# Last attention quad of a fused attention and MLP block: its own token order with large P·V groups, two more pieces of the output projection inside it

## Chip, core and metric

One core of one Trainium2 chip. The number that counts is the device time of one execution, in microseconds (us), as the median of the runs; less is better. TensorE multiplies matrices into PSUM, VectorE, ScalarE and GpSimd (POOL) work element by element, SyncE (SP) issues the transfers.

## What is computed

```python
h = _layernorm(x) * (1 + ca) + sa              # x: 2048 x 576, float32
q = (h @ wq) as 32 heads of 18;  k = h @ wk;  v = h @ wv      # one key and one value head for all
p = softmax(q k^T * 18 ** -0.5)
x = x + ga * ((p v as 2048 x 576) @ wo)
h = _layernorm(x) * (1 + cb) + sb
y = _layernorm(h)
x = x + gb * (gelu(y @ w1 + b1) @ w2 + b2)     # hidden size 4608
```

The six vectors sa, ca, ga, sb, cb, gb come from one small product of a conditioning vector.

## The kernel before, in words

The queries are cut into 4 blocks of 512 tokens and the heads into 8 groups of four, which makes 32 "quads" (n = 0 to 31). For each quad the kernel makes 64 score tiles of 128 keys by 512 queries (token S0 or S1, `st_mm` at line 927: one matmul into a PSUM bank, then one Exp on ScalarE into a tile P), and 64 unit products with V (token V with a number, `pv_mm` at line 914: four matmuls side by side on the columns of the array, one unit is 128 of 512 query columns). 16 chunks of 128 keys make a quad; the products with V run eight units behind the scores (`LAG`), so a quad's last two chunks are multiplied in the next quad. Beside this, a quad also makes the row maxima of the next quad (M and X/R tokens, on VectorE). The last quad has no next one, so it has no maxima.

Each engine runs its instructions in the order in which the program issues them, and that order is written out by hand as a string of tokens: `QUAD`, `QUADW`, and for the last quad `LAST` and `LASTW`, strung together in a loop (lines 894, 895 and 989). The loop at line 980 goes through the quads and walks their tokens. PSUM has 8 banks in this stage: `psB` four, `psM` three, `psC` one (the accumulator of P·V). A score tile takes the next bank of psB or psM, and TensorE can be at most as many scores ahead of ScalarE as there are banks.

After a quad's last P·V, `post_quad` (line 733) goes through five steps, one at each of the tokens T1, RC, T2, OS: ScalarE copies O out of psC, VectorE transposes it, the rows are divided by their sum, VectorE transposes back, and OS splits O into a high part (ScalarE, line 757) and a low part (line 758, POOL for all quads but the last) and sends both with four transfers (line 762) into the tile `ATT` (named big in the profile), which the output projection reads.

The output projection (`wo_mm`, line 711) makes 128 tokens by 288 columns per piece. Token WO runs one whole piece (14 matmuls) of the first three token blocks; 24 such pieces are spread over the later quads, the last two of them at the very end of quad 30 and in the middle of quad 31. The fourth block's pieces have five row groups k = 0 to 4 with three matmuls each; k = 0 to 3 need the quads up to 30, k = 4 only quad 31. They run in `wo_tile` (line 1065), which opens the MLP stage: three token tiles with k = 0 to 3 (72 matmuls) cover the five steps of the last quad, then k = 4 for the same tiles (18 matmuls), then the MLP's first products. During these steps `form` (line 1045) makes the MLP's operands: "+X" is a rounding copy on ScalarE, "=X" a difference on VectorE, "-X" the remainder on VectorE, which needs both. `todo` (line 1082) says which of them stand between the steps of the last quad.

Of the kernel before, what the change touches and what calls it, by code (L numbers as in the profile page):

```python
# [15 lines left out]
NB = 4  # L16
TB = S // NB
NT = TB // 128
KD = 5
NQ = H // 4  # L20
NQT = NB * NQ
# [11 lines left out]
def block_kernel(ctx: ExitStack, tc, x, wqkv, wo, w1, b1, w2, b2, c, wmod, ident_in, out):  # L33
    nc = tc.nc
    ve, ac, po, pe, sy = nc.vector, nc.scalar, nc.gpsimd, nc.tensor, nc.sync
# [15 lines left out]
    def psA(): return PS["t"].tile([128, 2, 512], F32, name="psA", bufs=2)  # L51
    def psM(): return PS["t"].tile([128, 512], F32, name="psM", bufs=3)
    def psB(): return PS["t"].tile([128, 512], F32, name="psB", bufs=PS["b"])
# [392 lines left out]
    for tb in range(NB):  # L446
        nz = big() if tb + 1 < NB else None
        for i, m in enumerate((4, 0, 1, 2, 3)):
# [27 lines left out]
            if tb < 2:  # L476
                for _ in range(NSTAT[tb][i]):
                    ln1_stats(*stats.popleft())
                for _ in range(NAPPLY[tb][i]):
                    b, t = applies.popleft()  # L480
# [13 lines left out]
    WO, YR, ATT, B2 = {}, {}, {}, {}  # L494
# [140 lines left out]
    def ln2_rows(tb, t):  # L635
        if "b" not in B2:
            B2["b"] = load_b2()
            yield
            b2_scaled(B2["b"])
        if tb % 2 == 0 and t == 0:  # L640
            YR[tb // 2] = per.tile([128, 2 * KD, TB], F32, name="yr", tag="big", bufs=3)
        yield from ln2_tile(tb, t)
        if tb % 2 and t == NT - 1:
            R = YR[tb // 2]
            po.tensor_tensor(R[:, 5:7], R[:, 7:9], R[:, 5:7], op=ALU.subtract)
            yield
            po.tensor_tensor(R[:, 5:7], R[:, 5:7], R[:, 0:2], op=ALU.add)
            yield
# [59 lines left out]
        po.tensor_tensor(R[:, 5:7], R[:, 5:7], R[:, 0:2], op=ALU.add)  # L708
        yield

    def wo_mm(tb, t, h2, p, k0, k1):
        A = ATT[tb]
        cs = slice(288 * h2, 288 * (h2 + 1))
        for k in range(k0, k1):
            w = 128 if k == KD - 1 and tb == NB - 1 else 126
            ah, al = (A[:w, i, 128 * t:128 * (t + 1)] for i in (k, KD + k))
            wh, wl = (WO[i][:w, k, cs] for i in "hl")
            if k < KD - 1 or tb == NB - 1:
                terms = [(ah, wh), (ah, wl), (al, wh)]
            else:  # L720
                terms = [(ah, wh), (al[:5 * DH], wl[:5 * DH])]
            for i, (a, b) in enumerate(terms):
                pe.matmul(p[:, :288], a, b, start=(k == 0 and i == 0), stop=(k == KD - 1 and i == len(terms) - 1))  # L723

    def wo_add(tb, t, h2, p):
        X = XT[:, NT * tb + t, 288 * h2:288 * (h2 + 1)]
        ve.tensor_tensor(X, p[:, :288], X, op=ALU.add)

    def wo_piece(tb, t, h2, p):
        wo_mm(tb, t, h2, p, 0, KD)  # L730
        wo_add(tb, t, h2, p)
# [46 lines left out]
    def load_w1(i, what):  # L778
        for w in what.split():
            a = 4 * OPS.index(w) if w in OPS else 28  # L780
            b = min(a + 4, 31)
            sy.dma_start(W1["r"][:, a:b].bitcast(F32), w1scr[i, :, a:b])
# [86 lines left out]
    def tail_parts(o, tail, d, e=po):  # L869

        e.tensor_tensor(d, tail[:, 0], tail[:, 1], op=ALU.subtract)
        for x, y in ((o[:, :2], tail), (o[:, 2], d)):
# [18 lines left out]
            M0 S1 OS S0 M1 WO S0 R1 M1 S0 M1 S0 X1 V3 S0 M1 M0 S1 S1 M1 S0 V3 M0 S1 S0 R1 S0 M0 X1 V3 M0 S1  # L891
            X1 M0 S1 M0 S1 V4 S1 M0 R1 S0 M1 S0 V4 S0 M1 M0 F1 S1 S0 S1 V4 M0 S1 M0 X1 S0 M1 F2 V4 M1 S0 S0
            S1 M0 S1 M0 V3 R1 S0 S0 S1 R1 M0 V3 S0 S1 M0 S1 M0 S1 V3 M0 S1 M1 S0 M1 S0 V3""".split()
    LASTW = "S0 S1 S0 S1 S0 S1 WO V4 S0 S1 V4".split()
    LAST = "S0 S1 S0 S1 V4 S0 S1 S0 S1 V4".split()
    P, PVt = {}, {}
    posts = []
    fill = deque([late_weights()])
# [1 line left out]
    def step(q):  # L900
        if q:
            try:
                return next(q[0])
            except StopIteration:
                q.popleft()
# [8 lines left out]
    def pv_mm(n, kc, h0, h1):  # L914

        if kc == 0 and h0 == 0:
            PVt[n] = psC()
        t = P.pop((n, kc)) if h1 == 4 else P[n, kc]
        cs = slice(128 * h0, 128 * h1)
        for j in range(4):  # L920
            pe.matmul(PVt[n][32 * j:32 * (j + 1), cs], V[:, kc, :], t[:, j, cs],  # L921
                      start=(kc == 0 and h0 == 0), stop=(kc == 15), skip_group_check=True)
        if kc == 15 and h1 == 4:
            posts.append(post_quad(n, PVt.pop(n)))
            next(posts[0])

    def st_mm(n, kc, g, i, ps):
        if (n, kc) not in P:
            P[n, kc] = pb.tile([128, 4, TB], F32, name="P", bufs=4)
        t = ps()  # L930
        pe.matmul(t, KS[64 * g:64 * g + 64, 128 * kc:128 * (kc + 1)], QST[n][64 * g:64 * g + 64, i, :],  # L931
                  start=True, stop=True)
        ac.activation(P[n, kc][:, 2 * i + g, :], t, AF.Exp, scale=SCALE)  # L933
# [21 lines left out]
    def between(n, kc):  # L955

        if kc == 1 and n >= 1 and n + 2 < NQT:
            load_q(n + 2)
        if kc % 2 and (held[0] != "T" or not pieces):
            held[0] = step(fill)  # L960
        if n > 3 and kc not in quiet:
            for _ in range(1 + (kc % 4 != 3)):
                step(prep)
        if kc == 8 and n == NQT - 1:
            while prep:
                step(prep)
# [3 lines left out]
    def wo_next(ps):  # L970
        tb, t, h2 = pieces.popleft()
        wo_piece(tb, t, h2, ps())
        for _ in range(2):
            if held[0] == "T":
                held[0] = step(fill)
        if h2 and tb < 2:
            fill.append(ln2_rows(tb, t))

    pq = 0
    for n in range(NQT):  # L980
        ns = [0, 0]
        if n < NQT - 1:
            order = QUADW if n > NQ else QUAD
            if n == NQT - 2:
                order = order + ["WO"]
        else:
            order = []
            for d in range(8):
                order += LASTW + ["RW"] if d == 4 else LAST
                order += {1: ["T1"], 2: ["RC"], 4: ["T2"], 5: ["OS", "V4"]}.get(d, [])  # L990
        if n < NQT - 1:
            kf, kr = (sum(int(tok[1]) for tok in order[:order.index(a)] if tok[0] == "V") // 4 for a in ("F2", "RC"))
            quiet = kf - 2, kf - 1, kr - 1
        for tok in order:
            if tok[0] == "V":
                g = int(tok[1])
                while g:
                    i = min(g, 4 - pq % 4)
                    if pq >= LAG:
                        pv_mm(*divmod((pq - LAG) // 4, 16), pq % 4, pq % 4 + i)  # L1000
                    pq, g = pq + i, g - i
                    if pq % 4 == 0:
                        between(*divmod(pq // 4 - 1, 16))
            elif tok[0] == "S":
                g = int(tok[1])
                st_mm(n, ns[g] // 2, g, ns[g] % 2, psM if ns[g] % 2 and (n == NQT - 1 or n == NQT - 2 and ns[g] > 24) else psB)
                ns[g] += 1
            elif tok in maxima:
                unit = next(maxima[tok], None)
                if unit:  # L1010
                    mx_mm(*unit, tok[0], int(tok[1]))
            elif tok == "WO":
                wo_next(psB)
            elif tok == "RW":
                for i, w in enumerate("hl"):
                    sy.dma_start(WO[w][:, KD - 1, :].bitcast(F32), woscr[i])
            elif tok[0] == "F":
                (smax_fin1 if tok == "F1" else smax_fin2)(n + 1)
            elif n:
                if next(posts[0], 0) == 0:  # L1020
                    posts.pop()
        if n == NQT - 1:
            W1["r"] = per.tile([128, 40, 128], F32R, name="w1a", tag="big", bufs=3)
            load_w1(0, " ".join(OPS) + " tails")
# [38 lines left out]
    wop = {}  # L1063

    def wo_tile(t, k0, k1):
        if t not in wop:
            p = psA() if t != 2 else None
            wop[t] = [psB()[:, :288] if t == 2 else p[:, h2, :288] for h2 in range(2)], p
        for h2 in range(2):
            wo_mm(NB - 1, t, h2, wop[t][0][h2], k0, k1)  # L1070
        if k1 == KD:
            o, p = wop[t]
            if p is None:
                for h2 in range(2):
                    wo_add(NB - 1, t, h2, o[h2])
            else:
                Xv = XT[:, NT * (NB - 1) + t, :].rearrange("p (a b) -> p a b", a=2)
                ve.tensor_tensor(Xv, p[:, :, :288], Xv, op=ALU.add)

    for t in range(3):  # L1080
        wo_tile(t, 0, KD - 1)
    todo = deque(("+B11 +T2", "-B11 =T3 +B21 +T3", "-T2 -T3", "-B21"))
    form(todo.popleft())
    for _ in posts.pop():
        form(todo.popleft())
# [7 lines left out]
    for t in range(3):  # L1093
        wo_tile(t, KD - 1, KD)
# [410 lines left out]
```

## Time and profile before

| | |
|---|---|
| median of 3 runs | 2228.65 us (2228.53 to 2231.1) |
| span of the profiled execution | 2225.7 us, 2.95 us under that median; the page gives no other time for it |
| TensorE busy | 2207.4 us (99%) |
| VectorE, ScalarE, POOL busy | 1931.9, 1639.8, 1527.0 us |
| Exp of the scores, ScalarE (L933) | 2008 of 621 ns |
| last quad | about 1337 to 1373.8 us in the span |

A busy TensorE is not a TensorE at its peak: a matmul counts as busy while it sits in the pipeline, so the table's 99% says little about a stage. In the rows, a number in brackets is the engine's idle time before the instruction and what released it; "x4" is a merged run of four instructions, whose time runs from the first start to the last end. PEld is the weight load that goes before each matmul; it waits where the matmul would.

### The profile page before, as it was taken

To read this page: it belongs to the slowest core of one execution; us is meant where nothing else is said; L and a number is where in the kernel's file an instruction comes from. 1 tells how busy PE (TensorE), PEld (TensorE's weight loads), DVE (VectorE), ACT (ScalarE), POOL (GpSimd) and SP (SyncE) were. 2 spreads that over 40 slices of the span, in tenths; PEclk is the share of its full clock that TensorE was granted. 3 is DMA by queue.
4 is the path that set the end of the run, shared out by engine and by line. 5 is a ranking of instruction groups with operands and counts; after the bars stand their busy time and mean duration, and the time that the engine had idled before them with its cause. 6 is when DMAs were issued, how large, how long until landed. Compare 5 with 4: busy or idle time off the path is not lost.

```text
span 2225.7 us, 46108 instructions
## 1 busy us (share of the span) xinstructions
PE 2207.4 (99%) x16630; PEld 1451.2 (65%) x16630; DVE 1931.9 (87%) x3415; ACT 1639.8 (74%) x3145; POOL 1527.0 (69%) x1761
## 2 busy tenths in 40 slices
PE   8999999999999999999999999999999999999999
PEld 6654544444544445454454545888888898989898
DVE  7589999999999999999999983887888878888887
ACT  5569999999999999999999997444444444343443
POOL 6653455666776687677676631888888867877776
PEclk9999999999999999999999999999999999999999
DMA  6232143433333333333333322666666646676664
GB/s 231 85 131 92 34 135 115 139 125 119 127 119 114 115 129 105 107 126 111 126 123 117 115 70 63 205 178 175 178 179 180 185 129 182 180 218 188 177 185 124
DMA packets 184776, 308.00 MB, mean 138 GB/s; under 512 B 19711, under 2 KB 75407, under 8 KB 184549
## 3 DMA queue, kind: packets, MB, share of 16 engines
q1 hardware_dynamic: 184405, 304.91, 44.3%
q8 instruction: 132, 2.16, 0.4%
q14 instruction: 95, 0.78, 0.1%
q10 hardware_dynamic: 144, 0.15, 0.0%
HBM read 200.97 MB, written 93.79 MB: 132 GB/s over the span
## 4 chain that ended last, share of the span: by engine, by line
PE 93%; ACT 1%; DVE 1%; issue 0%; ACTq 0%; DVEq 0%
PE psC L921 24%; PE psB L1144 18%; PE psA L1247 16%; PE psB L931 14%; PE psM L319 12%; PE psB L723 2%; PE psB L941 2%; PE psA L1281 1%; PE psA L723 1%; ACT P L933 1%; PE psB L155 0%; PE psB L248 0%; PE psB L357 0%; PE psM L931 0%; DVE mx L344 0%; DVE mx L337 0%
## 5 line engine op out<-in xcount | busy, mean ns | idle before, releaser
L933 ACT ACTIVATE P<-psB 128x512 f32<-128x512 f32 x2008 | 1051.1, 621 | 43.8 <-PE psM L319 20.0
L953 DVE TENSOR_REDUCE mx<-psM 128x1 f32<-128x512 f32 x1476 | 934.3, 682 | 29.9 <-PE psM L319 12.9
L931 PE MATMUL psB<-qst,KS 64*128 64x512 f32 x2008 | 603.5, 435 | 0.1
L319 PE MATMUL psM<-KS,qst 64*128 64x512 f32 x1722 | 591.2, 435 | 0.5 <-DVE mx L337 0.5
L921 PE MATMUL psC<-P,V 128*32 128x256 f32 (+3 forms) x6600 | 571.9, 440 | 0.5 <-ACT O L738 0.5
L931 PEld LDWEIGHTS psB<-qst,KS 64*128 64x128 f32 x2008 | 300.4, 184 | 225.6 <-ACT P L933 185.1
L319 PEld LDWEIGHTS psM<-KS,qst 64*128 64x128 f32 x1722 | 284.1, 184 | 185.6 <-DVE mx L953 130.2
L1144 PE MATMUL psB<-ops,w1a 128*128 128x512 f32 x1512 | 393.8, 396 | 0.2 <-DVE h L1159 0.2
L1144 PEld LDWEIGHTS psB<-ops,w1a 128*128 128x128 f32 x1512 | 270.1, 188 | 46.7 <-DVE h L1159 0.6
L921 PEld LDWEIGHTS psC<-P,V 128*32 128x32 f32 x6600 | 146.4, 108 | 185.3 <-issue 156.6
L1253 DVE TENSOR_TENSOR XT<-psA,XT 128x576 f32<-128x576 f32 x330 | 241.8, 753 | 18.6 <-PE psA L1247 13.2
L1247 PEld LDWEIGHTS psA<-w2s,big 128*128 128x128 f32 x1584 | 223.0, 188 | 14.0 <-POOL big L1221 2.5
L1247 PE MATMUL psA<-w2s,big 128*128 128x288 f32 x1584 | 230.5, 294 | 0.0
L1157 ACT ACTIVATE psB<-gs 128x512 f32<-128x512 f32 x144 | 86.7, 602 | 127.8 <-DVE gs L1156 127.7
L1221 POOL TENSOR_TENSOR big<-s,big 128x512 fp32r<-128x512 f32 x132 | 170.8, 1294 | 10.6
L951 DVE CUSTOM_DVE_ANT_0 xc<-psM,xc 128x512 f32<-128x512 f32 x246 | 166.3, 683 | 12.8 <-PE psB L931 6.4
L1153 ACT ACTIVATE h<-psB,b1t 128x512 f32<-128x512 f32 x144 | 97.9, 680 | 102.0 <-PE psB L1144 81.3
L758 POOL TENSOR_TENSOR os<-O,os 128x512 fp32r<-128x512 f32 x31 | 39.9, 1286 | 185.4 <-ACT os L757 185.4
L944 ACT ACTIVATE xc<-psB 128x512 f32<-128x512 f32 x246 | 154.7, 629 | 4.0 <-PE psB L941 1.4
L1156 DVE SCALAR_TENSOR_TENSOR gs<-psB,h 128x512 f32<-128x512 f32 x144 | 98.6, 685 | 39.8 <-ACT psB L1154 39.7
L792 POOL TENSOR_TENSOR r<-r,r 128x256 fp32r<-128x256 f32 (+1 forms) x162 | 121.8, 752 | 13.0
L1162 ACT ACTIVATE big<-h 128x512 fp32r<-128x512 f32 x39 | 24.7, 634 | 133.8 <-DVE h L1159 133.8
(212 smaller groups left out, 3326.8 us busy)
## 6 DMA issues: line engine op xcount, KB each, us to landing
w1a<-w1scr SPq DMA_DIRECT2D x252, 256.0 KB
w2s<-w2sum SPq DMA_DIRECT2D x132, 288.0 KB
w1scr<-r SPq DMA_DIRECT2D x126, 256.0 KB
w2s<-w2scr SPq DMA_DIRECT2D x76, 288.0 KB
w2scr<-r SPq DMA_DIRECT2D x72, 288.0 KB
w2sum<-r SPq DMA_DIRECT2D x72, 288.0 KB
qst<-qscr SPq DMA_DIRECT2D x192, 72.0 KB
w1a<-w2scr SPq DMA_DIRECT2D x33, 288.0 KB
```

The costliest lines, as they stand in the source:

```text
L319: pe.matmul(o, QST[n][64 * g:64 * g + 64, p, 128 * qt:128 * (qt + 1)], KS[64 * g:64 * g + 64, 512 * kb:512 * (kb + 1)], start=True, stop=True)
L792: po.tensor_tensor(o[:, n:2 * n], src, o[:, :n].bitcast(F32), op=ALU.subtract)
L921: pe.matmul(PVt[n][32 * j:32 * (j + 1), cs], V[:, kc, :], t[:, j, cs], start=(kc == 0 and h0 == 0), stop=(kc == 15), skip_group_check=True)
L931: pe.matmul(t, KS[64 * g:64 * g + 64, 128 * kc:128 * (kc + 1)], QST[n][64 * g:64 * g + 64, i, :], start=True, stop=True)
L933: ac.activation(P[n, kc][:, 2 * i + g, :], t, AF.Exp, scale=SCALE)
L944: ac.activation(XC[-1], t, AF.Relu)
L951: ve.tensor_tensor_reduce(c, t, c, 1.0, -3.0e38, ALU.add, ALU.max, o)
L953: ve.tensor_reduce(o, t, axis=AX.X, op=ALU.max)
L1144: pe.matmul(o, x, y, start=(first and i == 0), stop=(i == len(terms) - 1), skip_group_check=True)
L1221: po.tensor_tensor(unit(u, 1), x, unit(u, 0).bitcast(F32), op=ALU.subtract)
L1247: pe.matmul(p[:, i, :288], x[:, ts_], W2S[k][:, y], start=(bool(first) and q == 0), stop=(q == 2), skip_group_check=True)
L1253: ve.tensor_tensor(o, p[:, :, :288], o, op=ALU.add)
```

## The change

1. The last quad gets an order of its own (`LAST`), with the same 64 scores and the same 68 units of P·V, in groups of 8 to 12 units instead of 4 (one group of 2 stands behind an inserted piece, and 12 units with the 4 of the closing call follow the last scores).
2. Its scores take the seven banks of psB and psM in strict turn (4 to 3).
3. The WO piece at the end of quad 30 moves into quad 31, which now holds two.
4. A new token WP makes the fourth block's third token tile, k = 0 to 3, in the last quad: twice 12 matmuls, each with its own addition to x on VectorE. `wo_tile` then opens the MLP with two tiles (48 matmuls) and makes only k = 4 of the third.
5. `todo`: =T3, +T3, -T3, +B21 and -B21 all stand behind the second transpose of the last quad, ahead of its split.

```diff
@@ wo_mm @@
-    def wo_mm(tb, t, h2, p, k0, k1):
+    def wo_mm(tb, t, h2, p, k0, k1, end=KD, first=0):
...
-                pe.matmul(p[:, :288], a, b, start=(k == 0 and i == 0), stop=(k == KD - 1 and i == len(terms) - 1))
+                pe.matmul(p[:, :288], a, b, start=(k == first and i == 0), stop=(k == end - 1 and i == len(terms) - 1))
@@ token strings @@
-    LASTW = "S0 S1 S0 S1 S0 S1 WO V4 S0 S1 V4".split()
-    LAST = "S0 S1 S0 S1 V4 S0 S1 S0 S1 V4".split()
...
+            S1 WO RW S0 S1 S0 S1 S0 RC T2 S1 S0 V10 OS S1 S0 S1 S0 S1 S0 WP V2 S0 S1 S0 S1 S0 S1 V8 S0 S1 S1 S0
...
@@ the loop over quads @@
-            if n == NQT - 2:
-                order = order + ["WO"]
         else:
-            order = []
-            for d in range(8):
-                order += LASTW + ["RW"] if d == 4 else LAST
-                order += {1: ["T1"], 2: ["RC"], 4: ["T2"], 5: ["OS", "V4"]}.get(d, [])
+            order = LAST
...
-                st_mm(n, ns[g] // 2, g, ns[g] % 2, psM if ns[g] % 2 and (n == NQT - 1 or n == NQT - 2 and ns[g] > 24) else psB)
+                two = sum(ns) % 7 % 2 if n == NQT - 1 else ns[g] % 2 and n == NQT - 2 and ns[g] > 24
+                st_mm(n, ns[g] // 2, g, ns[g] % 2, psM if two else psB)
...
+            elif tok == "WP":
+                h2 = part.popleft()
+                p = psB()
+                wo_mm(NB - 1, 2, h2, p, 0, KD - 1, KD - 1)
+                wo_add(NB - 1, 2, h2, p)
@@ opening of the MLP stage @@
-            wo_mm(NB - 1, t, h2, wop[t][0][h2], k0, k1)
+            wo_mm(NB - 1, t, h2, wop[t][0][h2], k0, k1, first=KD - 1 if t == 2 else 0)
...
-    for t in range(3):
+    for t in range(2):
         wo_tile(t, 0, KD - 1)
-    todo = deque(("+B11 +T2", "-B11 =T3 +B21 +T3", "-T2 -T3", "-B21"))
+    todo = deque(("+B11 +T2", "-B11", "-T2", "=T3 +T3 -T3 +B21 -B21"))
```

How the orders stand, at two places. First TensorE at the seam between the last quad and the MLP stage, before: the last P·V, then the fourth block's pieces (psA). The names in brackets are what an instruction waits for: Activation is ScalarE, DMAHW1 to DMAHW6 are transfers, the last of which are the four that bring quad 30's O into the tile big.

```order
L921 MATMUL psC<-P,V 32x512 x3
L921 MATMUL psC<-P,V 32x512 [waits Activation_49] x5
L723 MATMUL psA<-wos,big 128x288 x9
L723 MATMUL psA<-wos,big 128x288 [waits DMAHW4_49,DMAHW5_49,DMAHW3_49,DMAHW6_49,DMAHW2_49,DMAHW1_49]
L723 MATMUL psA<-wos,big 128x288 x14
L723 MATMUL psA<-wos,big 128x288 [waits Activation_49]
```

And now, inside the last quad: the P·V group V10 behind which the OS step is issued, six scores, the first WP, V2.

```order
L922 MATMUL psC<-P,V 32x512 x8
L922 MATMUL psC<-P,V 32x256 [waits Activation_49]
...
L932 MATMUL psM<-qst,KS 128x512
L932 MATMUL psB<-qst,KS 128x512
L932 MATMUL psM<-qst,KS 128x512
L932 MATMUL psB<-qst,KS 128x512 [waits Activation_49]
L932 MATMUL psM<-qst,KS 128x512 [waits Activation_49]
L932 MATMUL psB<-qst,KS 128x512 [waits Activation_49]
L723 MATMUL psB<-wos,big 128x288 [waits Activation_49]
L723 MATMUL psB<-wos,big 128x288 x8
L723 MATMUL psB<-wos,big 128x288 [waits DMAHW4_49,DMAHW5_49,DMAHW3_49,DMAHW6_49,DMAHW2_49,DMAHW1_49]
L723 MATMUL psB<-wos,big 128x288 x2
L922 MATMUL psC<-P,V 32x256 x4
```

The wait for the same six transfers, on the tenth matmul of the fourth block's first piece, has moved from behind the last P·V to the place six scores after OS.

Second VectorE in the MLP's opening, before: the five steps of the last quad (L741, L744, L745, L747, L758) among the operand pieces (L1049 is "=", L1058 is "-").

```order
L741 STREAM_TRANSPOSE T<-O 128x512 [waits DVE_49,Activation_49]
...
L1049 TENSOR_TENSOR yr<-yr 128x1024 [waits DVE_49]
L744 RECIPROCAL R<-T 128x16
L745 TENSOR_TENSOR T<-T,R 128x512 [waits DVE_49]
L1058 TENSOR_TENSOR ops<-yr,ops 128x1024 [waits Activation_49] x2
L747 STREAM_TRANSPOSE O<-T 128x512 [waits DVE_49,Pool_49]
L1058 TENSOR_TENSOR ops<-yr,ops 128x1024
L758 TENSOR_TENSOR big<-O,big 128x512 [waits Activation_49]
```

And now (L1052 is "=", L1061 is "-").

```order
L741 STREAM_TRANSPOSE T<-O 128x512 [waits DVE_49,Activation_49]
...
L744 RECIPROCAL R<-T 128x16 [waits DVE_49]
L745 TENSOR_TENSOR T<-T,R 128x512 [waits DVE_49]
L1061 TENSOR_TENSOR ops<-yr,ops 128x1024 [waits Activation_49]
L747 STREAM_TRANSPOSE O<-T 128x512 [waits DVE_49,Pool_49]
L1052 TENSOR_TENSOR yr<-yr 128x1024
L1061 TENSOR_TENSOR ops<-yr,ops 128x1024 [waits Activation_49] x2
L758 TENSOR_TENSOR big<-O,big 128x512 [waits Activation_49]
```

The same instructions stand ahead of the split L758, but the difference "=T3", on which a ScalarE copy and then a remainder wait, has gone from the third place to behind the second transpose.

## Rows read from the trace of the kernel before

**Rows 1.** The page: span, and part 4, the chain by engine.

```profile
span 2225.7 us, 46108 instructions
...
PE 93%; ACT 1%; DVE 1%; issue 0%; ACTq 0%; DVEq 0%
```

**Rows 2.** Timeline of ScalarE, last quad: start us, us, engine, line, what, [idle before].

```profile
1336.59 0.75 ACT L933 ACTIVATE P<-psM 128x512 f32<-128x512 f32 x1
...
1338.45 1.09 ACT L933 ACTIVATE P<-psB 128x512 f32<-128x512 f32 x2 [1.11 <-PE psB L931]
...
1342.75 1.19 ACT L933 ACTIVATE P<-psB 128x512 f32<-128x512 f32 x2
...
1356.27 1.40 ACT L933 ACTIVATE P<-psB 128x512 f32<-128x512 f32 x2
1358.84 1.09 ACT L933 ACTIVATE P<-psM 128x512 f32<-128x512 f32 x2 [1.18 <-PE psM L931]
1360.34 1.08 ACT L933 ACTIVATE P<-psB 128x512 f32<-128x512 f32 x2 [0.41 <-PE psB L931]
...
1364.17 0.70 ACT L757 ACTIVATE os<-O 128x512 fp32r<-128x512 f32 x1
```

**Rows 3.** Timeline of TensorE, last quad.

```profile
1355.27 2.12 PE L723 MATMUL psB<-wos,big 126*128 126x288 f32 x14 [0.25 <-ACT P L933]
...
1359.74 0.51 PE L931 MATMUL psB<-qst,KS 64*128 64x512 f32 x2
...
1360.40 1.06 PE L921 MATMUL psC<-P,V 128*32 128x512 f32 x8
1361.40 0.50 PE L931 MATMUL psB<-qst,KS 64*128 64x512 f32 x2
...
1362.39 1.92 PE L921 MATMUL psC<-P,V 128*32 128x512 f32 x16
1364.25 0.50 PE L931 MATMUL psB<-qst,KS 64*128 64x512 f32 x2
```

**Rows 4.** Timelines of POOL and of SP's queue: the way of quad 30's O into big.

```profile
1364.95 1.28 POOL L758 TENSOR_TENSOR os<-O,os 128x512 fp32r<-128x512 f32 x1 [19.76 <-ACT os L757]
...
1366.26 3.34 SPq L762 DMA_DIRECT2D big<-os  x4
```

**Rows 5.** The DMA view of 1367 to 1371 us: busy tenths, 0.1 us each.

```profile
DMA  0000000545634000665442006554430054735699
```

**Rows 6.** TensorE's granted clock: weight loads, tables by time (PEclk third from right), a matmul group.

```profile
126.81 0.29 PEld L319 LDWEIGHTS psA<-KS,qst 64*128 64x128 f32 x3 [0.95 <-DVE mx L337]
...
130.00:130.50 0.50, 0.50 (x4) 0.20 (x3) 0.42 (x2) 0.41 (x1) 0.00 (x0) 0.53 0.92 238
...
136.50:137.00 0.50, 0.50 (x6) 0.43 (x4) 0.00 (x0) 0.00 (x0) 0.00 (x0) 0.64 1.09 410
...
1340.00:1344.00 4.00, 3.52 (x24) 0.98 (x21) 0.96 (x2) 4.00 (x10) 0.00 (x0) 1.00 0.00 0
...
134.68 1.93 PE L921 MATMUL psC<-P,V 128*32 128x512 f32 x8
```

**Rows 7.** Timeline of TensorE, the opening of the MLP stage.

```profile
1373.82 6.64 PE L723 MATMUL psA<-wos,big 126*128 126x288 f32 x48
1380.30 3.34 PE L723 MATMUL psB<-wos,big 126*128 126x288 f32 x24
1383.48 1.77 PE L723 MATMUL psA<-wos,big 128*128 128x288 f32 x12
```

**Rows 8.** Timelines of VectorE and ScalarE, the same opening.

```profile
1376.83 1.23 DVE L1049 TENSOR_TENSOR yr<-yr 128x1024 f32<-128x1024 f32 x1
...
1382.87 0.68 DVE L758 TENSOR_TENSOR big<-O,big 128x512 fp32r<-128x512 f32 x1
...
1378.09 1.06 ACT L1056 ACTIVATE ops<-yr 128x1024 fp32r<-128x1024 f32 x1 [0.66 <-DVE yr L1049]
1381.87 0.63 ACT L757 ACTIVATE big<-O 128x512 fp32r<-128x512 f32 x1 [2.72 <-DVE O L747]
```

More of the change, by code (lines that the diff above doesn't have):

```diff
@@ L893, in block_kernel @@
             S1 M0 S1 M0 V3 R1 S0 S0 S1 R1 M0 V3 S0 S1 M0 S1 M0 S1 V3 M0 S1 M1 S0 M1 S0 V3""".split()
-    LASTW = "S0 S1 S0 S1 S0 S1 WO V4 S0 S1 V4".split()
-    LAST = "S0 S1 S0 S1 V4 S0 S1 S0 S1 V4".split()
+    LAST = """S1 S0 S1 S0 V8 S0 S1 S0 S1 S0 S1 WO S0 S1 S0 S1 S1 S0 V9 S1 S0 S1 T1 S0 S1 S0 S1 V11 S0 S1 S0 S1 S0
+            S1 WO RW S0 S1 S0 S1 S0 RC T2 S1 S0 V10 OS S1 S0 S1 S0 S1 S0 WP V2 S0 S1 S0 S1 S0 S1 V8 S0 S1 S1 S0
+            S1 S0 V8 S1 S0 S1 S0 S0 S1 WP S0 S1 S0 S1 V12""".split()
     P, PVt = {}, {}
@@ L977, in wo_next @@
             fill.append(ln2_rows(tb, t))
+    part = deque((0, 1))
     pq = 0
@@ L995, in block_kernel @@
             if tok[0] == "V":
-                g = int(tok[1])
+                g = int(tok[1:])
                 while g:
```

## The prediction

> **What bounds the kernel now.** I read the page first, then the timelines of the stretch that the change touches. The chain that ended last is TensorE for 93% [rows 1], but that is the whole kernel; the last quad must be read by itself. The reader is to see two things there. First, ScalarE sets its pace: from 1342.75 to 1356.27 us it started 28 Exps, one every (1356.27 - 1342.75) / 28 = 0.483 us, without an idle time [rows 2], while TensorE has room: four scores take 1360.40 - 1359.74 = 0.66 us up to the P·V behind them and four units 1361.40 - 1360.40 = 1.00 us up to the next score [rows 3], 1.66 us against 4 x 0.483 = 1.93 us of Exp. Second, ScalarE runs dry only behind a WO piece: 1.11 us after the one that closes quad 30, 1.18 + 0.41 us after the one in the middle [rows 2], 2.70 us together. The opening of the MLP stage is TensorE's: 48 and 24 products, then k = 4, stand end to end [rows 7]. The last P·V ends at 1373.82 us; I call that point T.
>
> **The change part by part.** The sum is made against this execution, whose span of 2225.7 us lies 2.95 us under the median of 2228.65; the difference that comes out is added to the median.
>
> *Where the OS step comes.* Without a WO behind quad 30, ScalarE goes on from its last Exp there at 1336.59 us [rows 2]. Ahead of the OS copy stand that Exp, the 36 Exps of quad 31 that the new order puts there, and the copy of O, taken at one pitch: 38 x 0.483 = 18.35 us. Two WO pieces now stand behind six scores each and with all seven banks in turn; what ScalarE idles behind each has no row, so I bound it by 0 (the seven banks cover it) and 1.6 us (the old WO in this quad) and take 0.5 us, nearer to 0 because five or six Exps of 0.483 us are queued over a piece of 2.12 us [rows 3]. OS then starts at 1336.59 + 18.35 + 1.0 = 1355.9 us (1354.9 to 1358.1).
>
> *The first WP waits for it.* In quad 30's old place the copy starts at 1364.17 us [rows 2], POOL's remainder at 1364.95, the first of four transfers is issued at 1366.26 and the four take 3.34 us to issue [rows 4]; the DMA view shows them as four bursts, the last over at about 1370.8 us, where the next load joins [rows 5]. That is 6.6 us from copy to landing. None of it hangs on TensorE, and the queue ahead holds the same transfers as before, so it moves along: 1355.9 + 6.6 = 1362.5 us. The Trainium skill (DMA: Bandwidth & Descriptors, section Latency and other measured facts) gives about 0.6 us to the first byte of a transfer issued in this way; here the first burst begins at 1367.7, 1.4 us after the issue, and by the page the sum would be 0.8 us smaller; the row decides. TensorE gets to the tenth product of the first WP much earlier: six scores behind OS need only Exps that ran ahead of it, so WP starts some 0.2 us after OS, and nine products of 2.12 / 14 = 0.15 us take 1.4 us: 1357.5 us. **It stands for 5.0 us.** Everything behind it on TensorE stands too, and ScalarE, with six Exps queued, is dry after about 3 us. In the old kernel the same wait came after T, when the data had long landed.
>
> *From there to T.* Now TensorE has the longer list: 3 products 0.45; V2 0.5; three groups of six scores at 1.5 x 0.66 = 0.99, 2.97; V8 twice at 1364.25 - 1362.39 = 1.86, 3.72 [rows 3]; the second WP 12 x 0.15 = 1.8; four scores 0.66; the closing 16 units 2 x 1.86 = 3.72. Sum 13.8 us, against 22 Exps or 10.6 us on ScalarE. T comes at 1362.5 + 13.8 = 1376.3 us, **+2.5 us** (with OS at its bounds +1.5 to +4.7). The larger groups have their price in it: 8 units cost 1.86 instead of 2.00 us. I cost three edits at nothing: the new turn of the banks, under TensorE's longer list; the two extra additions of 128 x 288, on VectorE, which has hardly anything else in this quad; and the reload RW, which moves up with its WO piece and is wanted only at k = 4.
>
> *The clock.* Pauses of up to 0.95 us and thin work around 126 us were followed by a fall of the granted clock from 1.00 to 0.50 (2.4 to 1.2 GHz), from about 130.0 to 136.9 us [rows 6]. A group of four units took 1.93 us there against 1.06 [rows 3, 6], so such a stretch loses 45% of its work. A pause of 5 us is longer than any that I found between the kernel's first and last products, so I take it that the clock falls here as well. If the fall comes at the pause's start, 1.9 us of the 6.9 are left for work, if at its end all 6.9: 0.8 to 3.1 us lost, **+2.0 us**. A bound below that is nothing: from 1340 to 1344 us TensorE was idle for 0.48 us and the clock stayed at 1.00 [rows 6]. The Trainium skill (TensorE: Matmul & The Clock Gate, section HAM oscillation) says that a wait for a DMA between bursts sends the clock down and the next burst starts at the low level. By that rule the term stands; the fall at 130 us agrees with it, though it came after shorter waits.
>
> *The opening.* Before, 72 products reach from T to T + 9.66 us [rows 7], and the low half of the last quad's split is there at 1382.87 + 0.68 = T + 9.73 us [rows 8]: nothing waits. Now 48 products end at T + 6.48 us. The split does not come earlier. =T3 (1.23 us [rows 8]) is gone from the third place, so the second transpose is over 2.4 us sooner, but =T3, -T3 and -B21 now stand in a row behind it, and VectorE must stand through the copy +T3, 1.06 us on ScalarE plus its hand-overs [rows 8], since nothing else is left to put between. The high half waits behind +T3 and +B21 on ScalarE, to T + 9.5 us. VectorE's work ahead of the split is the same, plus that stop: T + 10.9 us. k = 4 goes on **1.2 us** later than before, and the 24 products that left (3.3 us [rows 7]) have bought only a pause, of 3.0 and 1.2 us with two products between. Its bounds are -3.3 us, if the split were there in time, and +1.5 with slow hand-overs; I take the order's. A second fall of the clock after it costs 1.2 to 3.1 us by the same reckoning, **+2.1 us**.
>
> Behind that, the MLP runs as before, with TensorE its bound, so nothing gives the time back. Sum: 2.5 + 2.0 + 1.2 + 2.1 = **+7.8 us**, or 2228.65 + 7.8 = 2236.5 us: case A, both waits and a fall of the clock after each. A measurement of this kernel can tell about 0.2%, 4.5 us, from no change.
>
> **The rivals.** A itself gets a chance of 0.46.
> - *Both waits, one fall*: 3.7 + 2.0 = +5.7 us, 2234.4 us. For it: the second pause is broken by two products. Chance 0.22.
> - *Both waits, no fall*: 2.5 + 1.2 = +3.7 us, 2232.4 us. For it: the 0.48 us near 1342 left the clock at 1.00 [rows 6]. Against it: that is a tenth of the pause here. Chance 0.14.
> - *The wait at WP is covered* (other side). Place: the tenth product of the first WP. It decides when quad 30's O lands less than some 3 us after the OS copy begins, the time for which ScalarE has Exps queued. Then of 2.70 us idle about 1.0 us is left, -1.7, and with the opening's +1.2 it is -0.5 us, or +1.6 with a fall there: about 2228.5 us. For it: everything else in the order fits, seven banks over a piece of 2.12 us. Against it: POOL's remainder alone ends 1364.95 + 1.28 - 1364.17 = 2.06 us after the copy's start, and four transfers are then still to be issued [rows 4]. Chance 0.12.
> - *Both waits are covered and all idle time goes*: -2.7 - 3.3 = -6.0 us, 2222.7 us. It needs the split by T + 6.5 us as well, which the order of VectorE's work excludes unless its pieces are much shorter. Chance 0.06.
>
> **How the numbers follow.** The likeliest case gives the number, 2236.5 us; by its terms' bounds (1.5 + 0.8 + 1.2 + 1.2 and 4.7 + 3.1 + 1.5 + 3.1) A lies between 2233.3 and 2241.0. The range goes from 2229.5, so that it takes in the cases with fewer falls, to 2240.5; the faster case (0.06), most of the covered one (0.09) and all terms at their upper ends at once are left out, not over 0.2 in all. Slower by over 4.5 us: A 0.46, nearly all of one fall 0.20, and 0.04 of no fall, 0.70. Faster by as much: 0.06. The rest, 0.24, is no change.
>
> **What would show it.** In the changed kernel's trace: the tenth product of the first WP should stand some 5 us with a transfer as the releaser, ScalarE should be dry for 4 to 5 us soon after the OS copy, and the last P·V should end 3 to 6 us later than 1373.82 us. Behind 48 products, k = 4 should stand about 4 us and the split's remainder on VectorE should end about 11 us after T. The granted clock should show 0.50 after one or both. I am wrong if the transfers land within 3 us of the copy, if the clock holds 1.00 through both pauses, or if the split is there before T + 8 us.

## The result, and the profile after

The changed kernel takes 2238.2 us (median of 5 runs, 2236.27 to 2238.58), the kernel before, on the same chip, 2228.53 us (5 runs, the three of the table before among them). The ratio is 1.004, with a 95% interval from 1.0028 to 1.0052: 9.7 us slower, where 7.8 us were forecast. The profiled execution has a span 10.5 us longer than that of before. (Below, one execution of e3 took 5102.56 us; its row in the table is of its other four.) The page of the changed kernel, span and chain:

```profile
span 2236.2 us, 46135 instructions
...
PE 95%; DVE 1%; ACT 1%; DMA 1%; POOL 1%; issue 1%; SPq 0%; ACTq 0%; POOLq 0%; DVEq 0%
```

A transfer now has its 1% in the chain, but the page says no more than that. To split the 10.5 us I use three instructions that both traces have. Q is the start of the last P·V group with quad 30's scores, T the start of the fourth block's 48 products, which is the end of the last P·V in the prediction, and S the start of the second run of MLP products (L1144 before, L1147 after; the line moves with each edit). Q to T is the last quad, T to S the opening of the MLP. Timeline of TensorE before, Q and S (T is in [rows 7]):

```profile
1335.09 0.85 PE L921 MATMUL psC<-P,V 128*32 128x384 f32 x8
...
1388.88 1.56 PE L1144 MATMUL psB<-ops,w1a 128*128 128x512 f32 x6
```

The same timeline of the changed kernel, with Q first and S last:

```profile
1336.05 0.85 PE L922 MATMUL psC<-P,V 128*32 128x384 f32 x8
...
1357.57 1.47 PE L723 MATMUL psB<-wos,big 126*128 126x288 f32 x9
1364.45 1.06 PE L723 MATMUL psB<-wos,big 126*128 126x288 f32 x3 [5.41 <-DMA big<-os]
...
1368.03 2.71 PE L922 MATMUL psC<-P,V 128*32 128x512 f32 x16
...
1380.82 6.64 PE L723 MATMUL psA<-wos,big 126*128 126x288 f32 x48
1390.27 0.85 PE L723 MATMUL psA<-wos,big 128*128 128x288 f32 x2 [2.81 <-ACT big L757]
1391.79 2.77 PE L723 MATMUL psA<-wos,big 128*128 128x288 f32 x10 [0.68 <-DVE big L758]
...
1399.33 1.57 PE L1147 MATMUL psB<-ops,w1a 128*128 128x512 f32 x6
```

Q to T has grown from 38.73 to 44.77 us (+6.04), T to S from 15.06 to 18.51 us (+3.45). The other 0.96 us were there at Q, before anything that the change touches. Both forecast waits stand in these rows: the first WP has nine products, then 5.41 us for the transfers of quad 30's O; and behind the 48 products, where [rows 7] show none, 2.81 us and, two products later, 0.68 us for the split.

ScalarE in the same quad runs dry 1.8 us into TensorE's wait (the last Exp ends at 1360.80 us, the wait begins at 1359.04); these rows of its timeline are the OS copy, the last two Exps that had a score, and the next ones:

```profile
1357.16 0.69 ACT L757 ACTIVATE os<-O 128x512 fp32r<-128x512 f32 x1
...
1359.59 0.71 ACT L934 ACTIVATE P<-psM 128x512 f32<-128x512 f32 x1
1360.07 0.73 ACT L934 ACTIVATE P<-psB 128x512 f32<-128x512 f32 x1
1367.28 0.60 ACT L934 ACTIVATE P<-psB 128x512 f32<-128x512 f32 x1 [6.48 <-PE psM L932]
```

The way of O from that copy, in the timeline of POOL:

```profile
1357.93 1.29 POOL L758 TENSOR_TENSOR os<-O,os 128x512 fp32r<-128x512 f32 x1 [2.74 <-ACT os L757]
```

In that of SP's queue:

```profile
1359.24 3.33 SPq L762 DMA_DIRECT2D big<-os  x4
```

And in the DMA view of 1360 to 1366 us (busy tenths, 0.15 us each):

```profile
DMA  0000255430464410555304545992499999999779
```

Issue comes 2.08 us after the copy and takes 3.33 us, as in [rows 4]. The fourth burst is over at about 1363.75 us, where the next load joins: 6.6 us after the copy, as I read it from [rows 4, 5]. But the tenth product starts only 0.7 us later still, 7.29 us after the copy.

TensorE's granted clock (third column from the right) in tables by time of the changed kernel:

```profile
1362.00:1370.00 8.00, 5.55 (x29) 2.29 (x33) 0.46 (x1) 2.72 (x6) 0.00 (x0) 0.57 0.82 268
1380.00:1387.00 7.00, 7.00 (x58) 6.18 (x47) 5.00 (x7) 2.50 (x3) 0.00 (x0) 1.00 0.00 0
1390.00:1397.00 7.00, 6.05 (x21) 5.50 (x22) 5.24 (x9) 1.25 (x3) 1.59 (x2) 0.51 0.17 42
```

As around 130 us in [rows 6], it fell to 0.50 (1.2 GHz): late in the first wait and again at the end of the wait in the opening, for some 6.8 us each time, and in both places TensorE then had work: a P·V group of eight units took 2.71 us across the end of the first fall, where 1.86 us is the price at full clock [rows 3].

### The profile page after: what moved, and what is told of

Read it like the earlier page. It is cut to its first block, busy times and chain, and to the rows that moved or that the text cites. A ratio compares the mean times of both kernels' runs of the same rounds, so it can differ in the third digit from the quotient of the medians.

```text
span 2236.2 us, 46135 instructions
## 1 busy us (share of the span) xinstructions
PE 2208.7 (99%) x16646; PEld 1454.4 (65%) x16646; DVE 1932.1 (86%) x3417; ACT 1642.8 (73%) x3145; POOL 1527.6 (68%) x1761
## 4 chain that ended last, share of the span: by engine, by line
PE 95%; DVE 1%; ACT 1%; DMA 1%; POOL 1%; issue 1%; SPq 0%; ACTq 0%; POOLq 0%; DVEq 0%
PE psC L922 24%; PE psB L1147 18%; PE psA L1250 16%; PE psB L932 14%; PE psM L319 13%; PE psB L723 2%; PE psB L248 2%; PE psB L942 2%; PE psA L1284 1%; PE psA L319 1%; PE psB L155 1%; DMA bigw<-in_wqkv 1%; DVE mx L344 0%; ACT P L934 0%; PE psA L723 0%
## 5 line engine op out<-in xcount | busy, mean ns | idle before, releaser
L1147 PE MATMUL psB<-ops,w1a 128*128 128x512 f32 x1512 | 394.4, 396 | 0.2 <-DVE h L1162 0.2
L1147 PEld LDWEIGHTS psB<-ops,w1a 128*128 128x128 f32 x1512 | 270.7, 188 | 46.8 <-DVE h L1162 0.6
L758 POOL TENSOR_TENSOR os<-O,os 128x512 fp32r<-128x512 f32 x31 | 39.9, 1286 | 167.5 <-ACT os L757 167.5
```

What stands on the lines that cost most here:

```text
L1147: pe.matmul(o, x, y, start=(first and i == 0), stop=(i == len(terms) - 1), skip_group_check=True)
```

## The experiments

All runs in one table. The columns Q to T and T to S are differences of rows as above, from one profiled execution each; "against before" is the difference of the medians on the same chip. The intervals of e1 and e7 hold 1: these two can't be told from the kernel before.

| kernel | median us | against before us | ratio, 95% interval | Q to T us | T to S us |
|---|---|---|---|---|---|
| before | 2228.53 | | | 38.73 | 15.06 |
| the change | 2238.2 | +9.7 | 1.004 [1.0028, 1.0052] | 44.77 | 18.51 |
| e1 early OS | 2229.47 | +2.0 | 1.0008 [0.9999, 1.0017] | 37.30 | 18.54 |
| e2 old todo | 2235.12 | +7.6 | 1.0033 [1.002, 1.0046] | 44.75 | 16.39 |
| e3 split first | 2236.97 | +9.5 | 1.0046 [1.003, 1.0062] | 44.57 | 15.95 |
| e4 fill at WP | 2233.56 | +6.1 | 1.0027 [1.0015, 1.0039] | 42.52 | 17.72 |
| e5 order alone | 2225.93 | -2.5 | 0.9989 [0.998, 0.9998] | 36.47 | 15.06 |
| e6 opening, GpSimd | 2226.1 | -2.3 | 0.999 [0.9981, 0.9998] | 37.29 | 12.37 |
| e7 early OS, old todo | 2227.86 | -0.5 | 0.9995 [0.9986, 1.0004] | 37.30 | 16.64 |
| e8 OS six earlier | 2233.27 | +4.9 | 1.002 [1.0011, 1.0029] | 40.92 | 18.22 |
| e9 opening mended | 2223.67 | -4.2 | 0.9981 [0.9973, 0.999] | 37.30 | 12.39 |
| e10 fill in the opening | 2234.85 | +7.0 | 1.0028 [1.0016, 1.004] | 45.12 | 16.18 |

### The wait at the first WP

**e1** takes the cause away: quad 30's four later steps move up by whole groups, so that O lands before the first WP, which stays where it is. **e8** moves OS up by six scores only, with RC and T2 ahead of it, so that part of the wait stays.

```diff
 e1
-S1 S0 S1 S0 V8 S0 S1 S0 S1 S0 S1 WO S0 S1 S0 S1 S1 S0 V9 S1 S0 S1 T1 S0 S1 S0 S1 V11 S0 S1 S0 S1 S0
-S1 WO RW S0 S1 S0 S1 S0 RC T2 S1 S0 V10 OS S1 S0 S1 S0 S1 S0 WP V2
+S1 S0 S1 S0 V8 T1 S0 S1 S0 S1 S0 S1 RC T2 WO S0 S1 S0 S1 S1 S0 V9 OS S1 S0 S1 S0 S1 S0 S1 V11 S0 S1 S0 S1 S0
+S1 WO RW S0 S1 S0 S1 S0 S1 S0 V10 S1 S0 S1 S0 S1 S0 WP V2
 e8
-T1 S0 S1 S0 S1 V11 S0 S1 S0 S1 S0 S1 WO RW S0 S1 S0 S1 S0 RC T2 S1 S0 V10 OS
+T1 S0 S1 S0 S1 V11 RC T2 S0 S1 S0 S1 S0 S1 WO RW S0 OS S1 S0 S1 S0 S1 S0 V10
```

> The changed kernel, but the five steps of quad 30's P·V stand earlier in the last quad's order (T1 behind V8, RC and T2 ahead of the first WO, OS behind V9), so that its transfers are issued some 18 Exps earlier; scores, P·V groups and both WP stay where they are. My theory (the first WP waits for the transfers, and the clock falls in that pause): the wait of 5.4 us and the low clock behind it are gone, the last P·V ends about 1 us before that of the kernel before instead of 6 us behind it, and the time comes down by about 7 us against the changed kernel, to 2231 us; the pause in the opening stays. Rival (the large P·V groups starve ScalarE, and the wait only takes time that would have been lost in any case): the gain is 3 us or less, and ScalarE shows gaps behind the V9 to V11 groups that add up to several us.

> The changed kernel with OS six scores earlier (RC and T2 move ahead with it), all else as changed. My theory: the transfers land 2.9 us sooner, the first WP waits some 2.5 us instead of 5.4, and the last P·V ends 2.9 us sooner if the clock still falls in the shorter pause, 5 us sooner if it stays at 1.00. Rival (the wait is not for the split's place but for SP's queue, which holds the transfers back behind the reload RW): the wait shrinks by 1 us or less.

Measured. In e1's timeline of TensorE, Q and T:

```profile
1334.11 0.85 PE L922 MATMUL psC<-P,V 128*32 128x384 f32 x8
...
1371.41 6.64 PE L723 MATMUL psA<-wos,big 126*128 126x288 f32 x48
```

The last quad takes 37.30 us, 7.47 less than in the change and 1.43 less than before; the wait is gone, and e1's clock table holds 1.00 up to T. T to S stays at 18.54. ScalarE's gaps up to T are 0.18, 0.20 and 0.15 us, so the rival, that the large groups starve it, falls. So the place of these steps alone, against the place of WP, costs 7.5 us. e8 leaves this at WP, in the same timeline:

```profile
1359.64 0.85 PE L723 MATMUL psB<-wos,big 126*128 126x288 f32 x3 [2.13 <-DMA big<-os]
```

and in its clock table:

```profile
1360.00:1361.00 1.00, 1.00 (x11) 0.35 (x9) 0.46 (x1) 0.00 (x0) 0.00 (x0) 0.50 0.92 338
...
1364.00:1365.00 1.00, 1.00 (x14) 0.14 (x6) 0.00 (x0) 1.00 (x3) 0.00 (x0) 1.00 0.95 360
```

3.28 us less wait brought 3.85 us, so the rival, a queue that holds the transfers back, falls. The clock fell after this shorter pause too, for some 3.4 us instead of 6.8.

**e4** leaves the wait and gives TensorE something to do in it: 36 products whose results nobody reads, between the ninth and the tenth product of the first WP.

```diff
-wo_mm(NB - 1, 2, h2, p, 0, KD - 1, KD - 1)
+wo_mm(NB - 1, 2, h2, p, 0, KD - 2, KD - 1)
+if not h2:
+    z = psB()
+    for _ in range(4):
+        wo_mm(NB - 1, 2, h2, z, 0, KD - 2, KD - 2)
+wo_mm(NB - 1, 2, h2, p, KD - 2, KD - 1, KD - 1)
```

> The changed kernel with 36 added products (the first nine of the first WP four times more, into a PSUM bank that nothing reads) between the ninth and the tenth product of the first WP, where TensorE waits for the transfers; 5.0 us at 0.14 us each. My theory (the low clock behind the pause costs 2 us or more of its own): TensorE works through the pause, the clock stays at 1.00 there, and although work was added the last P·V ends 2 to 2.5 us sooner. Rival (the time is the pause alone, and the low clock is hidden under ScalarE's Exps): no change, or slower by what the added products overrun.

Its timeline of TensorE:

```profile
1356.65 6.37 PE L723 MATMUL psB<-wos,big 126*128 126x288 f32 x45
1363.55 0.63 PE L723 MATMUL psB<-wos,big 126*128 126x288 f32 x3 [0.54 <-DMA big<-os]
...
1377.70 6.64 PE L723 MATMUL psA<-wos,big 126*128 126x288 f32 x48
```

Its clock table, through the wait and behind it:

```profile
1356.00:1364.00 8.00, 7.46 (x54) 6.72 (x52) 0.00 (x0) 3.88 (x8) 1.29 (x1) 1.00 0.28 71
1364.00:1370.00 6.00, 6.00 (x54) 2.00 (x52) 0.46 (x1) 4.78 (x10) 0.00 (x0) 1.00 0.82 295
```

From the end of the wait to T it takes 1377.70 - 1363.55 = 14.15 us; in the change the same list takes 1380.82 - 1364.45 = 16.37. The lists hold the same work, the clock differs: **the fall cost 2.22 us there**. With 36 products more, the quad is 2.25 us shorter (42.52). The median is 3.6 us nearer to that of before than the changed kernel's, but the two intervals overlap: the price rests on the rows. (Another 0.79 us came in the opening, which this edit does not touch: behind pauses of 2.80 and 1.00 us the low stretch was some 3.4 us in this execution.) The Trainium skill (TensorE: Matmul & The Clock Gate, section HAM oscillation) says that waits for transfers between bursts send the clock down; by that rule the fall came, and the trace agrees: 0.50 behind the idle wait, 1.00 behind the filled one.

### The opening

**e2** undoes part 5 alone; **e7** does so beside e1's order.

```diff
-todo = deque(("+B11 +T2", "-B11", "-T2", "=T3 +T3 -T3 +B21 -B21"))
+todo = deque(("+B11 +T2", "-B11 =T3 +B21 +T3", "-T2 -T3", "-B21"))
```

> The changed kernel with the old order of the operand pieces between the steps of the last quad (part 5 of the change undone). My theory: the low half of the last split is there 9.7 us after the last P·V instead of 10.9, the pause behind the 48 products is about 3.2 us instead of 3.5 to 4.2, and 1.2 us are saved; the clock still falls in the pause. Rival (the order of these pieces does not matter, since the pause comes from the 24 products that left): no change.

> The changed kernel with both repairs: quad 30's steps early, and the old operand order. My theory (the two losses lie one behind the other and add up): 1.4 us gained in the quad, 1.3 us lost in the opening, together the time of the kernel before within 0.5 us, and the opening still shows a pause of some 2.7 us behind the 48 products with the low clock for a few us. Rival (the pause in the opening takes back what the quad gains whatever its length, as the first experiment's is 3.5): 2 us or more slower than before.

In e2's timeline of TensorE, k = 4:

```profile
1387.66 0.53 PE L723 MATMUL psA<-wos,big 128*128 128x288 f32 x2 [2.19 <-ACT big L757]
1388.70 2.77 PE L723 MATMUL psA<-wos,big 128*128 128x288 f32 x10 [0.52 <-DVE big L758]
```

T to S is 16.39 us in e2 and 16.64 in e7: part 5 costs about 2.0 us, and without it the two tiles still lose 1.3 to 1.6 us against the three of before. The 2.0 us are more than the 1.2 of e2's theory: the pause came down from 3.49 to 2.71 us (the theory had 3.2), and the low stretch behind it was shorter too, some 3.4 us. e7 shows both repairs together, as its theory said: no pause in the quad, and the time of the kernel before. The why of part 5 is in the changed kernel's timeline of VectorE:

```profile
1386.47 1.18 DVE L1052 TENSOR_TENSOR yr<-yr 128x1024 f32<-128x1024 f32 x1
1388.78 2.36 DVE L1061 TENSOR_TENSOR ops<-yr,ops 128x1024 fp32r<-128x1024 f32 x2 [1.12 <-ACT ops L1059]
1391.06 0.68 DVE L758 TENSOR_TENSOR big<-O,big 128x512 fp32r<-128x512 f32 x1
```

=T3, a stop of 1.12 us for the copy +T3, then two remainders, and only then the split: it ends at 1391.74, T + 10.9 us, the forecast figure.

**e3** puts these pieces behind the split.

```diff
+todo = deque(("+B11 +T2", "-B11", "-T2", "", "=T3 +T3 -T3 +B21 -B21"))
```

> The changed kernel, but =T3, +T3, -T3, +B21 and -B21 stand behind the last quad's split instead of ahead of it. My theory (the split is late by its place in the order, and the clock falls in that pause): the split is there about 7 us after the last P·V, the 48 products cover all but some 0.5 us, the clock stays at 1.00 in the opening, and about 4 us of pause plus 2 us of low clock are saved, 6 us against the changed kernel. Rival (the operand pieces then come too late for the MLP's third product, which needs T3): k = 4 starts as early, but a wait for T3's remainder gives back 2 us or more, and the gain is under 4 us.

Its timeline of TensorE, from T on:

```profile
1379.62 6.97 PE L723 MATMUL psA<-wos,big 126*128 126x288 f32 x50
1386.79 1.59 PE L723 MATMUL psA<-wos,big 128*128 128x288 f32 x10 [0.20 <-DVE big L758]
...
1393.88 1.85 PE L723 MATMUL psA<-wos,big 126*128 126x288 f32 x12 [3.30 <-DVE XT L1081]
```

The run of 50 holds the 48 products and the first two of k = 4; the next ten follow 0.20 us later, 7.2 us behind T. But the next tile needs the bank that the first addition to x frees, and on VectorE this addition is queued behind the pieces moved there:

```profile
1386.04 0.69 DVE L758 TENSOR_TENSOR big<-O,big 128x512 fp32r<-128x512 f32 x1 [0.70 <-ACT big L757]
...
1393.08 1.41 DVE L1081 TENSOR_TENSOR XT<-psA,XT 128x576 f32<-128x576 f32 x2
```

TensorE's pause has moved by one step and is nearly as long as the first, 3.30 us. The clock held, though; the clock table inside the pause and behind it:

```profile
1391.00:1392.00 1.00, 0.00 (x0) 0.00 (x0) 1.00 (x2) 0.00 (x0) 1.00 (x1) 1.00 0.37 55
...
1394.00:1395.00 1.00, 1.00 (x8) 1.00 (x9) 1.00 (x3) 0.00 (x0) 0.68 (x1) 1.00 0.00 0
```

S is 2.6 us nearer to T than in the change, not the 6 us of the theory; the rival's "under 4 us" came, with a wait for the first addition in place of T3's remainder. The median shows no gain; the profiled execution is the fastest of the runs, and what takes the time back in the others is not in this trace; whether the clock fell in their pause is not known.

**e6** keeps e1's order and leaves only =T3 between the split and the additions; -B21, =T1 and =T4 go to GpSimd, the rest stays on VectorE behind the additions. In this kernel the operand T4 is made from a row that =T1 has changed already, so that part of what it computes is not the reference's; kinds and sizes of the instructions are the same.

```diff
-form = op_pieces(YR[0], ve)
+form = op_pieces(YR[0], po)
-todo = deque(("+B11 +T2", "-B11", "-T2", "=T3 +T3 -T3 +B21 -B21"))
+todo = deque(("+B11 +T2", "-B11", "-T2", ""))
...
-for w in todo:
-    form(w)
+form("+B21 =T3 +T3 -B21")
...
-form("+t0 -t0")
...
-form("+t1 =T4 =T1 +T1 -t1 -T1")
+form("-T3 +t0 -t0 +t1 =T1 +T1 -t1 -T1 =T4")
```

> A version that may beat both: quad 30's steps early, both WP kept, and the opening in another order: the last quad's split before all of T3 and B21, =T3 alone between the split and the additions to x, -B21, =T1 and =T4 on POOL. My theory (the 24 products that left the opening are worth their 3.3 us once the split no longer stands behind operand pieces and the bank is free in time): k = 4 starts about 7 us after the last P·V without a pause over 0.5 us, the clock stays at 1.00, and the MLP's second product starts 12 to 13 us after the last P·V instead of 15.1 in the kernel before: with 1.4 us from the quad 3 to 4.5 us faster than before. Rival (VectorE's work sets the opening, wherever its pieces stand): the second product starts early, but the products behind it wait for the operands or for u, and the gain against the kernel before is 1.5 us or less.

T to S falls to 12.37 us, but of the 4.1 us that the two columns give together the median keeps 2.3, short of the theory's 3 to 4.5. In the timeline of TensorE, POOL is the releaser:

```profile
1395.32 1.44 PE L1145 MATMUL psB<-ops,w1a 128*128 128x512 f32 x5 [1.73 <-POOL ops L1061]
```

The timeline of POOL:

```profile
1382.28 6.20 POOL L1052 TENSOR_TENSOR yr<-yr 128x1024 f32<-128x1024 f32 x2
...
1392.90 4.71 POOL L1061 TENSOR_TENSOR ops<-yr,ops 128x1024 fp32r<-128x1024 f32 x2
```

Two differences take 3.10 us each on POOL, 1.23 on VectorE [rows 8]; the remainder that waits behind them comes too late.

**e9** is e6 with the two differences back on VectorE and in the right order; only -B21 is on GpSimd.

```diff
-    at = {"B11": (0, 0, ve), "B21": (2, 2, e2), ...
+    at = {"B11": (0, 0, ve), "B21": (2, 2, e3 or e2), ...
-form = op_pieces(YR[0], ve)
+form = op_pieces(YR[0], ve, po)
...
+form("-T3 +t0 -t0 +t1 =T4 =T1 +T1 -t1 -T1")
```

> Edit: quad 30's softmax sums, reciprocals and operand copies go early as in e1, so that neither WP piece waits; in the opening the split follows the end of attention at once, =T3 is the only piece between it and the additions to x, and the other seven pieces follow the additions on VectorE, but for -B21, which goes to GpSimd. Theory (the opening is set by the wait of the fourth row tile's low-half operand and by the bank that waits for the first addition to x): the interval from the last quad-30 product group to the end of attention 37.3 us as in e1, the fourth tile's products 7 us behind the end of attention without a pause, clock 1.00 there, the MLP's second product about 12.4 us behind the end of attention (15.06 before the change, 18.51 in it), no wait for GpSimd as in e6; 3 to 4 us faster than the kernel before. Rival (VectorE's seven pieces set the opening wherever they stand): the second product starts early as well, but later products wait for additions and operand pieces behind them on VectorE, and at most 1.5 us is left.

Timeline of TensorE from T to S:

```profile
1370.99 6.97 PE L723 MATMUL psA<-wos,big 126*128 126x288 f32 x50
1378.17 1.61 PE L723 MATMUL psA<-wos,big 128*128 128x288 f32 x10 [0.20 <-DVE big L758]
...
1383.38 1.57 PE L1145 MATMUL psB<-ops,w1a 128*128 128x512 f32 x6
```

And the table of the stretch:

```profile
1371.00:1390.00 19.00, 18.62 (x123) 17.10 (x120) 16.57 (x19) 8.85 (x12) 7.55 (x4) 1.00 0.19 59
```

The theory holds and its rival falls: TensorE is busy 18.62 of 19 us, the clock is 1.00, T to S is 12.39 us, and up to 1425 us nothing on TensorE waits for POOL. It has the lowest time against before of all versions here, 4.2 us faster (interval 2.2 to 6.0 us), which is as the two columns say: 1.43 + 2.67 = 4.1 us.

**e10** prices the second fall as e4 priced the first: the changed kernel with 27 products more, unread, behind the 48.

```diff
 for t in range(2):
     wo_tile(t, 0, KD - 1)
+z = psB()
+for _ in range(3):
+    wo_mm(NB - 1, 0, 0, z, 0, KD - 2, KD - 2)
```

> Edit: the changed kernel with 27 products more, whose results nobody reads, put into a free bank between the 48 products behind the end of attention and the fourth row tile's products, which wait there for the split. They take about 3.65 us, near the 3.5 us of that pause. Theory (the low clock behind the pause costs about 2.1 us of the opening): the clock stays at 1.00 in the opening, the MLP's second product starts about 16.3 us behind the end of attention instead of 18.5, and the kernel is about 2 us faster than the changed kernel though it does more work. Rival (the low clock lies under VectorE's work there and costs nothing): the second product starts 18.5 us or later behind the end of attention, and the time is the changed kernel's or up to 0.5 us more.

Timeline of TensorE from T to S:

```profile
1381.15 6.62 PE L723 MATMUL psA<-wos,big 126*128 126x288 f32 x48
1387.60 3.75 PE L723 MATMUL psB<-wos,big 126*128 126x288 f32 x27
1391.19 0.42 PE L723 MATMUL psA<-wos,big 128*128 128x288 f32 x2
...
1397.33 1.57 PE L1150 MATMUL psB<-ops,w1a 128*128 128x512 f32 x6
```

The clock behind the filled pause:

```profile
1390.00:1397.00 7.00, 6.49 (x45) 5.98 (x44) 6.64 (x10) 1.59 (x4) 1.48 (x1) 1.00 0.16 48
```

T to S is 16.18 us instead of 18.51, so **the second fall cost 2.33 us**, although k = 4 itself starts 0.6 us later than in the change. The medians against before point the same way, +7.0 against +9.7 us, with intervals that overlap.

### The new order without the extra pieces

**e5** keeps the large groups, the strict turn of the banks, both WO pieces in the quad and e1's early steps, and drops WP: the opening has three tiles and its old todo again.

```diff
-... WP V2 ... S0 S1 WP S0 S1 S0 S1 V12
+... V2 ... S0 S1 S0 S1 S0 S1 V12
-first=KD - 1 if t == 2 else 0
+first=0
-for t in range(2):
+for t in range(3):
```

> Of the change only the last quad's order (parts 1 to 3) is kept, with quad 30's steps early as in the first experiment; no WP, three token tiles in the opening, the old operand order. My theory (the order by itself pays, what was put into it does not): no wait for a transfer, no low clock, the opening is as before, and the last P·V ends 1.4 to 2.5 us sooner, so 1.5 to 2.5 us faster than the kernel before. Rival (the opening's pause belongs to the new order, since P·V's last group of 16 ends in another way): the opening keeps 1 us or more of its loss, and the time is no better than before.

Q to T is 36.47 us, 2.26 less than before, T to S 15.06, as before; the median is 2.5 us below before's. Behind the two WO pieces e5's ScalarE shows gaps of 0.19 and 0.20 us; that leaves 2.31 of the 2.70 us of [rows 2] as gain, near the 2.26. Which of the three parts brings how much of it was not tried one by one. And e1 against e5 gives the price of the two WP in the quad: 0.83 us, for 24 products that take 3.34 us in the opening [rows 7].

## Why the prediction was right, and where it was off

The sign and both mechanisms hold: case A, two waits with a fall of the clock after each. The sum was +7.8 us, the two intervals show 6.04 + 3.45 = +9.49, the medians +9.7. Term by term, times in the quad shifted by the 0.96 us at Q:

| term | forecast us | measured us | from |
|---|---|---|---|
| start of the OS copy | 1355.9 | 1356.2 | 1357.16 - 0.96 |
| copy to the tenth product | 6.6 | 7.29 | 1364.45 - 1357.16 |
| tenth product to T at full clock | 13.8 | 14.15 | e4 |
| first fall | 2.0 | 2.22 | the change against e4 |
| opening at full clock, against before | +1.2 | +1.12 | e10: 16.18 - 15.06 |
| second fall | 2.1 | 2.33 | the change against e10 |

- **The wait at WP** was the mis-sized step, +4.5 us with its fall where 6.04 came. Four small misses in one direction: 0.3 + 0.69 + 0.35 + 0.22 = 1.56 us. The largest is the landing. I read its end from the last busy tenth of the DMA strip [rows 5], and a product that waits starts 0.7 us behind that. In the old kernel no engine stood at this transfer, so the strip was all there was; it is a lower bound. The 7.29 us are no accident of one execution: from the copy to the tenth product it is 7.28 us in e2, 7.30 in e4 and 7.21 in e8.
- **ScalarE's pace** held in its sum, 19.61 us from quad 30's last Exp (1337.55) to the copy, forecast 19.35; in part that is luck. It idled 0.18 + 0.20 = 0.38 us behind the two WO pieces where I took 1.0, and the 38 starts took (19.61 - 0.38) / 38 = 0.506 us each where I took 0.483: two misses, 0.6 and 0.9 us, of opposite sign.
- **The clock** fell behind both pauses, as I took it; that the fall is paid for, and does not lie under another engine's work, is shown by e4 and e10. That the second fall came, and at its full length, is in part luck: behind the same pause of the opening the low stretch was 3.4 us in e4, and behind 3.30 us in e3 there was none.
- **The opening** came out by its own steps: the split's end at T + 10.9 us, +1.12 us before the clock. That the 24 products "bought only a pause" is true of this order of VectorE's work alone. e9 shows what they buy when the split goes first and the additions second: 2.67 us.
- **The rivals.** One fall and no fall are out by the clock tables; both covered and faster, which I gave 0.06, did not come, but e9 shows that it lay within reach of two more edits: 1.43 us of the quad and 2.67 of the opening.
- What gained is hidden in the sum: the order itself, with quad 30's steps early, is worth 2.3 us (e5), and the WP products cost 0.83 us in the quad instead of 3.34. The change lost this, and 9.5 us more, nearly all of it to data that was late at two places.
- The 0.96 us at Q are not explained. They lie ahead of all that was changed; e1 and e2 had Q about 1 us sooner than before's, with the changed kernel's code up to there, so this is how executions scatter.

## What to carry to other kernels

Work that is moved into an idle stretch takes its inputs' due times with it: before moving it, look up when each input lands where it now stands, and move the producing steps first (one string of tokens was worth 7.5 us here). Where work is taken out of a stretch that covered another engine, that engine's chain must be shortened in the same edit, down to the buffer that the next step needs. And a pause on TensorE costs more than its length when the clock falls behind it; if the pause can't be removed, products that nobody reads can win back what the low clock takes, 2.2 to 2.3 us of the stretch in e4 and e10.

## What the runs showed that was not expected

- The clock also fell behind shorter pauses than the 5 us of the forecast: after 2.13 us in e8, and in e2 after 2.19 us and two products. The low stretches there were shorter, some 3.4 us instead of 6.8. But the length of the pause alone does not decide: e4's opening had 3.4 us behind pauses of 2.80 and 1.00 us, the change's 6.8 behind 2.81 and 0.68, and e3's pause of 3.30 us left the clock at 1.00. What decides is not shown here.
- Added work shortened a stretch: 36 products took 2.25 us off the quad (e4), 27 took 2.33 us off the opening (e10).
- GpSimd's difference of 128x1024 took 3.1 us beside 1.23 on VectorE (e6). With one such piece more on GpSimd nothing on TensorE waited for it (e9), with three it did (e6).
